# A chunked linear recurrence with both heads of a pair on the partition halves: one state scan, one masked copy, 64x64 matmuls, and two PSUM banks as one buffer

## The chip, the cores and the metric

The kernel runs on one core of one Trainium2 chip. The metric is the device time of the whole launch in microseconds (us), as a median over runs. Engines are named as in the profile: PE is the tensor engine's matmuls, PEld its weight loads, DVE the vector engine, ACT the scalar engine, POOL GpSimd, SP the queue that issues DMAs. L393 is line 393 of the kernel before.

## The reference

A recurrence over 768 time steps (batch 4, 8 heads of 48 columns) feeds a causal attention layer with four experts, of which each token uses two.

```python
for t in range(S):                                   # S = 768, D = 48
    cur = einsum('bhd,bhe->bhde', u[None] * kt, vt)
    y[:, :, t] = einsum('bhd,bhde->bhe', rt, state + cur)
    state = wt[:, :, :, None] * state + einsum('bhd,bhe->bhde', kt, vt)
x = y.transpose(0, 2, 1, 3).reshape(B, S, H * D)     # [4, 768, 384]
logits = x @ w_gate; topk = the two largest; w = softmax over the two
for e in range(4):
    q, k, v = x @ wq[e], x @ wk[e], x @ wv[e]        # 64 columns each
    a = softmax of the causal scores q k' / 8
    out += (gate of e, if chosen) * (a @ v @ wo[e])
```

## The kernel before

**Staging.** A unit is one batch and one half (g = 0 or 1) of its 768 steps: eight units. For each unit `rwkv` computes the recurrence and leaves its output, transposed and split into two parts (`xh`, `xl`); `moe` then does the attention of that half's queries. The recurrence of a unit is meant to run beside the attention of the unit before it. `rwkv` handles the heads in four pairs per unit, so 32 pairs in all, and cuts a half sequence into six chunks of 64 steps.

**Order.** Nothing is issued in program order. Every step is put into a `Plan` with an expected cost per engine, the tiles it reads and writes, and a wanted time (`want`, shifted by a table `OFF`). `Plan.order` then lets each engine take, of the steps whose inputs and buffers are free, the one that is wanted first, and emits the instructions in the order so found. Each engine executes its own list in that fixed order and waits on semaphores. All loads and stores are issued by SP, in order. Buffers are counted in `BUFS`; PSUM has eight banks: `sc` two buffers of two banks (scores), `mo` two of one bank (attention), `rw` two of one bank (recurrence). In the last unit's attention, when no recurrence is left, `mbank` hands out `rw` buffers as well as `mo` buffers, alternately.

**One pair, before** (all in `rwkv`). Head 0 lies on partitions 0 to 47, head 1 on 64 to 111 of a column-per-token layout. `suf` (L345) and `pre` (L349) are scans over the decays on 128 partitions. `kt` (L354) is the decayed keys. `mr` (L358) multiplies the receptances into `pre` twice, each time for 64 partitions: head 0 into the tile `pre`, head 1 into `mB`. `ktp` (L383) transposes the keys on PE and `kts` copies them to SBUF. `aps` (L393, L394) is twelve 64x64 products, two heads by six chunks: head 0's rows go to the lower half of one bank's partitions and head 1's rows to the upper, that is each head crosses to the other half. `am` (L397) copies them with the causal mask, head 0's to the free half of `pre`, head 1's to the free half of `mB`: two DVE instructions of 64 partitions. So `pre` holds, one above the other, what head 0 multiplies with the state and with the values, and `mB` the same for head 1.

`ups` (L409, L410) is what each chunk adds to the state: two blocks (`a` = 0, 1, the partition half of the tokens), each with a bank of its own and six products, and `us` copies each bank to `ust`. `ys` (L417) scans the state over the chunks, one DVE scan per head: into the upper or lower part of `ysA` and `ysB`, whose other part holds the values, laid out to match and loaded from `vY` by two DMAs. `carry` (L421, L424) hands the last state to the other half (g = 0, a DVE copy per head) or clears it (g = 1, a POOL memset per head). `yps` (L433, L434) is the output: twelve products with all 128 (or 112) rows, which read `ysA` and `ysB` with a step of eight floats per column. `addy` (L441) adds it to `xn`. After four pairs, `xp` (L454) transposes `xn` in three steps, each with a bank of `rw`. A product of float32 operands appears in the trace as two weight loads and two matmuls, so twelve products are 24 matmul rows.

Of the kernel before, what the change touches and what calls it, by code (L numbers as in the profile page):

```python
# [20 lines left out]
C = 64  # L21
# [9 lines left out]
# Time of an instruction by its shape, in ns: what the order of the instructions is planned with.  # L31
# [16 lines left out]
class Slot:  # L48
    """A buffer of a tag; which one, the plan says. It is made when the first instruction that needs it is emitted."""
# [11 lines left out]
# Time from the end of an instruction to the start of one on another engine that waits for it.  # L61
# [5 lines left out]
class Plan:  # L67
    """Orders instructions: each engine takes, of those whose inputs and tiles are there, the one that is
    wanted first. The instructions are then emitted by the time at which they started."""
# [5 lines left out]
    def add(self, kind, engs, fn, r=(), w=(), want=None):  # L75
        """engs: {engine: ns}; fn(engine) emits. r, w: what is read and written, Slots or (Slot, part)."""
# [23 lines left out]
    def order(self, free, slack=60.0, width=40):  # L100
# [7 lines left out]
        bufs = {}       # tag -> for each buffer, by when each engine is through with it; None while held  # L108
# [15 lines left out]
        while len(done) < len(ops):  # L124
            best = None
            for e in engines:
                c, t0 = [], 1e30
                for want, n in cand[e][:width]:
                    o = ops[n]
                    t = max(free[e], after(o["ready"], e))  # L130
                    for s in o["slots"]:
# [6 lines left out]
                        elif s.bank:        # two engines don't use a bank at once  # L138
                            t = max(t, after(s.ends, e, e))
# [42 lines left out]
def rwkv_moe(ctx: ExitStack, tc: tile.TileContext, wkr, vY, nat, uN,  # L182
# [12 lines left out]
    def bank(tag, name, dt=F32):  # L195
        w = 2048 // mybir.dt.size(dt) * (2 if tag == "sc" else 1)
        return Slot(ps, [128, w], dt, BANK.get(tag, tag), name, True)
# [26 lines left out]
    act = cst.tile([128, 1], F32, name="act")       # loads the table of the exponential  # L224
# [6 lines left out]
    # the scan over chunks, a row for each column of the state: the state that enters, what the chunks  # L231
    # add, a zero that ends the row; and the decays that follow them
# [25 lines left out]
    sel = cst.tile([NG, 3 * E, HD], BF16, name="sel")   # picks the two experts of a pair out of the gates  # L258
    tri = cst.tile([128, E, E], F32, name="tri")        # [e, e2]: 1 where e2 < e
# [13 lines left out]
    def weights(n, src, cols):  # L273
        """A matrix split exactly into two float32r parts."""
# [12 lines left out]
    def rwkv(b, g, v0, v1):  # L287
# [10 lines left out]
        for p in range(NP):  # L298
# [36 lines left out]
            mB = sb([128, NH, C], F32, "mB", f"mB{n}")  # L335
# [3 lines left out]
            def sfv(suf=suf):  # L339
# [4 lines left out]
            # suffix products inside each chunk, scanned from its end; column 0 of a block: the whole chunk  # L344
# [6 lines left out]
                [(lt, 0), "inv_pre"], [(pre, 0), (pre, 1)])  # L351
# [27 lines left out]
            ktp = bank("rw", f"ktp{n}")  # L379
# [7 lines left out]
            aps = bank("rw", f"aps{n}")  # L387
# [445 lines left out]
```

## Time and profile before

| | before |
|---|---|
| median of 3 runs | 500.53 us (499.93 to 500.97) |
| profiled execution, first to last instruction | 500.3 us |
| PE busy | 450.2 us (90%) |
| DVE busy | 425.7 us (85%) |
| ACT busy | 248.0 us (50%) |
| POOL busy | 170.5 us (34%) |
| mean granted TensorE clock | 0.942 of 2.4 GHz |
| DMA | 46.64 MB, 93 GB/s over the span |

The profiled execution has no time of its own beside its span; the span lies 0.2 us under the median of the timed runs. Busy times count overlapping instructions of one engine once. Matmuls are pipelined: a row's length is its latency, and the distance from one start to the next is what it costs in a stream. The kernel falls into three stretches: a start to about 50 us, a middle in which recurrence and attention run together, and from about 436 us the last unit's attention alone.

### The profile page before, as it was taken

To read this page: it belongs to the slowest core of one execution; us is meant where nothing else is said; L and a number is where in the kernel's file an instruction comes from. 1 tells how busy PE (TensorE), PEld (TensorE's weight loads), DVE (VectorE), ACT (ScalarE), POOL (GpSimd) and SP (SyncE) were. 2 spreads that over 40 slices of the span, in tenths; PEclk is the share of its full clock that TensorE was granted. 3 is DMA by queue.
4 is the path that set the end of the run, shared out by engine and by line. 5 is a ranking of instruction groups with operands and counts; after the bars stand their busy time and mean duration, and the time that the engine had idled before them with its cause. 6 is when DMAs were issued, how large, how long until landed. Compare 5 with 4: busy or idle time off the path is not lost.

```text
span 500.3 us, 10885 instructions
## 1 busy us (share of the span) xinstructions
PE 450.2 (90%) x4191; PEld 332.7 (66%) x4196; DVE 425.7 (85%) x866; ACT 248.0 (50%) x609; POOL 170.5 (34%) x218
## 2 busy tenths in 40 slices
PE   6867797999898998999988988999997989999985
PEld 3545676667766766767766666776766658886654
DVE  7999999969979899989999889989998876766561
ACT  3232545544445644655553734655552734575552
POOL 4555744412454244722234243722233240000000
PEclk9795899959898999999998999999997999999999
DMA  7544534222523323522331233522342110100101
GB/s 243 192 152 137 162 101 137 67 96 67 164 63 103 100 91 92 163 85 69 120 111 64 85 101 99 162 84 70 100 129 64 37 54 17 48 0 1 48 1 47
DMA packets 18564, 46.64 MB, mean 93 GB/s; under 512 B 2512, under 2 KB 9936, under 8 KB 18512
## 3 DMA queue, kind: packets, MB, share of 16 engines
q1 hardware_dynamic: 18512, 45.94, 29.5%
q8 instruction: 33, 0.54, 0.5%
q14 instruction: 19, 0.16, 0.1%
HBM read 41.21 MB, written 4.72 MB: 92 GB/s over the span
## 4 chain that ended last, share of the span: by engine, by line
PE 54%; DVE 34%; issue 5%; DMA 3%; ACT 2%; POOL 1%; SPq 0%; DVEq 0%; ACTq 0%; POOLq 0%
PE sp L589 8%; PE pp L500 7%; PE tp L609 6%; PE sp L588 6%; DVE ysB L417 5%; PE vp L530 4%; DVE pre L349 4%; DVE suf L345 4%; PE yp L632 3%; DVE ysA L417 3%; PE op L696 3%; PE sp L590 3%; PE aps L393 2%; DVE mx L594 2%; PE ups L409 2%
## 5 line engine op out<-in xcount | busy, mean ns | idle before, releaser
L596 ACT ACTIVATE a<-sp,mx 128x512 f32<-128x512 f32 (+5 forms) x96 | 60.8, 634 | 46.8 <-DVE mx L594 40.1
L594 DVE TENSOR_REDUCE mx<-sp 128x1 f32<-128x512 f32 (+5 forms) x96 | 58.8, 619 | 23.4 <-PE sp L590 22.6
L609 PE MATMUL tp<-ident,a 128*128 128x128 f32 x336 | 57.4, 290 | 7.3 <-ACT a L596 4.0
L354 POOL TENSOR_TENSOR kt<-lt,suf 128x384 f32<-128x384 f32 x31 | 33.7, 1087 | 81.8 <-PE aps L394 56.6
L201 ACT COPY ATa<-tp 128x512 f32<-128x512 f32 (+3 forms) x73 | 34.6, 477 | 42.7 <-PE tp L609 42.3
L589 PE MATMUL sp<-KS,QL 64*128 64x384 f32 (+4 forms) x128 | 54.7, 427 | 0.0
L588 PE MATMUL sp<-KS,QD 128*128 128x384 f32 (+4 forms) x128 | 51.4, 402 | 0.8 <-ACT a L596 0.5
L609 PEld LDWEIGHTS tp<-ident,a 128*128 128x128 f32 x336 | 39.2, 146 | 13.7 <-ACT a L596 5.4
L433 PE MATMUL yps<-ysA,pre 128*64 128x48 f32 x384 | 39.6, 276 | 7.9 <-issue 4.6
L500 PE MATMUL pp<-xh,wh_qk 128*128 128x384 f32 x96 | 40.8, 425 | 3.8 <-DVE QL L511 3.8
L374 POOL TENSOR_TENSOR xn<-nat,rk 128x144 f32<-128x144 f32 x42 | 29.9, 720 | 38.8 <-DVE rk L370 38.6
L434 PE MATMUL yps<-ysB,mB 112*64 112x48 f32 x384 | 37.9, 275 | 4.1 <-DVE ysB L417 4.1
L589 PEld LDWEIGHTS sp<-KS,QL 64*128 64x128 f32 x128 | 23.9, 187 | 23.1 <-issue 20.1
L364 POOL TENSOR_TENSOR nat<-nat,u_sb 128x288 f32<-128x288 f32 x30 | 26.6, 886 | 36.5 <-DMA nat<-in_nat_dram 20.7
L433 PEld LDWEIGHTS yps<-ysA,pre 128*64 128x64 f32 x384 | 29.5, 154 | 14.1 <-issue 8.4
L358 POOL TENSOR_TENSOR pre<-lt,pre 64x384 f32<-64x384 f32 x25 | 28.5, 1140 | 26.9 <-DVE pre L349 14.0
L409 PE MATMUL ups<-nat,kts 64*64 64x48 f32 x384 | 33.9, 229 | 2.5 <-DVE mB L397 1.2
L632 PE MATMUL yp<-ATa,v_sb 128*64 128x384 f32 (+2 forms) x224 | 35.9, 449 | 0.1
L345 DVE TENSOR_TENSOR_SCAN suf<-lt,one_suf 128x390 f32<-128x390 f32 x32 | 34.6, 1080 | 1.7 <-DMA lt<-in_wkr_dram 1.3
L509 ACT ACTIVATE QD<-pp 64x384 fp32r<-64x384 f32 x64 | 31.0, 484 | 9.1 <-PE pp L500 7.6
L409 PEld LDWEIGHTS ups<-nat,kts 64*64 64x64 f32 x384 | 26.8, 139 | 13.0 <-issue 6.2
L417 DVE TENSOR_TENSOR_SCAN ysB<-ust,wdec 48x384 f32<-48x384 f32 x32 | 34.6, 1082 | 1.0
(137 smaller groups left out, 1200.0 us busy)
## 6 DMA issues: line engine op xcount, KB each, us to landing
lt<-in_wkr_dram SPq DMA_DIRECT2D x31, 579.5 KB, 3.8
nat<-in_nat_dram SPq DMA_DIRECT2D x32, 432.0 KB, 3.3
out_dram<-ob SPq DMA_DIRECT2D x24, 192.0 KB, 1.9
ysB<-in_vY_dram SPq DMA_DIRECT2D x32, 96.0 KB, 2.5
ysA<-in_vY_dram SPq DMA_DIRECT2D x32, 96.0 KB, 2.6
w_qk<-in_wqk_dram SPq DMA_DIRECT2D x1, 768.0 KB, 4.5
w_vg<-in_wvg_dram SPq DMA_DIRECT2D x1, 390.0 KB, 4.5
lt<-in_wkr_dram SPq DMA_DIRECT2D x1, 384.0 KB, 3.2
```

The lines of the kernel that those rows point to most:

```text
L345: plan.add("suf", {"DVE": t_dve(WB)}, lambda e, suf=suf, w_=w_: nc.vector.tensor_tensor_scan(rev(suf()), rev(w_()), rev(one_suf), 0.0, op0 ...
L409: nc.tensor.matmul(ups()[0:64, o], kts()[q, i, 0:64], vn()[q, i, 0:D], start=True, stop=True)
L417: plan.add("ys", {"DVE": t_dve(D * NX)}, lambda e, rows=rows, ys=ys, us=us, wd=wd: nc.vector.tensor_tensor_scan(flat(ys()[rows]), flat(us[ ...
L433: nc.tensor.matmul(yps()[q, o:o + D], pre()[:, c, 0:C], ysA()[:, :, c], start=True, stop=True)
L434: nc.tensor.matmul(yps()[q, o + D:o + 2 * D], mB()[0:112, c, :], ysB()[0:112, :, c], start=True, stop=True)
L500: nc.tensor.matmul(pp()[:, 0:384], w[:, qk, k, cs], x()[:, k, :], start=(k == j == 0), stop=(k == j == 2))
L588: nc.tensor.matmul(spv()[:, h, :], QD[x]()[:, t], ks[:, o], start=True, stop=False)
L589: nc.tensor.matmul(spv()[:, h, :], QL[x // 2]()[hi, t], ks[hi, o], start=False, stop=h < np_ - 1)
L594: plan.add("max", {"DVE": t_dve(n)}, lambda e: nc.vector.tensor_reduce(mx(), spv(), axis=AX.XY, op=ALU.max, negate=True), [sp], [mx])
L596: plan.add("exp", {"ACT": t_exp(n)}, lambda e: nc.scalar.activation(a()[:, 0:n].rearrange("p (a n) -> p a n", a=np_), spv(), AF.Exp, bias= ...
L609: nc.tensor.transpose(tp()[:, j * 128:(j + 1) * 128], a()[:, (j0 + j) * 128:(j0 + j + 1) * 128], ident)
L632: nc.tensor.matmul(yp()[e * 64:e * 64 + 64, lo:384], v_sb[ep]()[:, j, e * 64:e * 64 + 64], at, start=(j == 0), stop=(j == nj - 1))
```

## The change

Both heads stay on their own partition halves. `mr` becomes one instruction on 128 partitions, in `pre`. `aps` keeps head 0 in the upper and head 1 in the lower half of the partitions; `am` is one instruction of 128 partitions into a tile of its own, `am`. `ups` is one block of twelve products into two banks, its products alternating between the partition halves of the tokens, and `us` one copy of 288 columns instead of two of 144. `ys` is one scan over 112 partitions into one tile, and `carry` one instruction. The values are loaded by one DMA into `vy`, contiguous by chunk. `yps` is 24 products, of 64 (or 48) rows and 64 output rows: for each chunk and head one with the state and one with the values, accumulated in PSUM, head 0 in the first of two banks and head 1 in the second. The recurrence's two one-bank buffers `rw` become one two-bank buffer `rw2`, which `ktp`, `aps`, `ups`, `yps` and `xp` take in turn, and which `mbank` lends out in the last unit. Three planned costs are new constants. `OFF`, `LEAD` and the other tables stay; the planned order follows from the new steps.

```diff
-        w = 2048 // mybir.dt.size(dt) * (2 if tag == "sc" else 1)
+        w = 2048 // mybir.dt.size(dt) * (2 if tag in ("sc", "rw2") else 1)
...
-            ysA = sb([128, D, NX], F32, "ysA", f"ysA{n}")
-            ysB = sb([128, D, NX], F32, "ysB", f"ysB{n}")
-            load("ldv", lambda t=ysB: flat(t()[0:64]), vY[b, g, p, 0:64], -1, [(ysB, "v")])
-            load("ldv", lambda t=ysA: flat(t()[64:128]), vY[b, g, p, 64:128], -1, [(ysA, "v")])
+            ys = sb([128, D, NX], F32, "ys", f"ys{n}")
+            vy = sb([128, NH, D], F32, "vy", f"vy{n}")
+            load("ldv", lambda vy=vy: flat(vy()), vY[b, g, p], NH * D, [vy])
...
-            for rows, m in ((slice(0, 64), pre), (slice(64, 128), mB)):
-                h = rows.start // 64
-                plan.add("mr", prod(384), lambda e, m=m, rows=rows, r_=r_, pre=pre: E_[e].tensor_tensor(
-                    m()[rows, :, 0:C], r_()[rows], pre()[rows, :, 0:C], op=ALU.mult),
-                    [(lt, 1), (pre, h)], [(m, h)])
+            plan.add("mr", prod(384), lambda e, r_=r_, pre=pre: E_[e].tensor_tensor(
+                pre()[:, :, 0:C], r_(), pre()[:, :, 0:C], op=ALU.mult), [(lt, 1), pre], [pre])
...
-                    nc.tensor.matmul(a_[64:128, o], k[0:64, c, :], mA[0:64, c, 0:C], start=True, stop=True)
-                    nc.tensor.matmul(a_[0:64, o], k[64:128, c, :], mB()[64:128, c, :], start=True, stop=True)
-            plan.add("aps", {"PE": 12 * 81}, amat, [kt, (pre, 0), (mB, 1)], [aps])
-            for rows, m, h in ((slice(64, 128), pre, 1), (slice(0, 64), mB, 0)):
-                plan.add("am", {"DVE": t_dve(384)}, lambda e, rows=rows, m=m, aps=aps: nc.vector.tensor_tensor(
-                    m()[rows, :, 0:C], aps()[rows, 0:NH * C].rearrange("p (c j) -> p c j", j=C),
-                    dec_mask[rows, None, :].to_broadcast([64, NH, C]), op=ALU.mult), [aps], [(m, h)])
+                    for h in range(2):
+                        nc.tensor.matmul(a_[half(h), c * C:(c + 1) * C], k[half(h), c, :], m[half(h), c, 0:C],
+                                         start=True, stop=True)
+            plan.add("aps", {"PE": T_APS}, amat, [kt, pre], [aps])
+            plan.add("am", {"DVE": t_dve(384)}, lambda e, am=am, aps=aps: nc.vector.tensor_tensor(
+                am(), aps()[:, 0:NH * C].rearrange("p (c j) -> p c j", j=C),
+                dec_mask[:, None, :].to_broadcast([128, NH, C]), op=ALU.mult), [aps], [am])
...
-            for a in range(2):
-                ups = bank("rw", f"ups{n}{a}")
+            ups = bank("rw2", f"ups{n}")
+            def states(e, ups=ups, kts=kts, vn=vn):
+                for i in range(3):
+                    for a in range(2):
+                        o = slice(a * 512 + i * D, a * 512 + (i + 1) * D)
+                        nc.tensor.matmul(ups()[0:64, o], kts()[half(a), i, 0:64], vn()[half(a), i, 0:D], start=True, stop=True)
+                        nc.tensor.matmul(ups()[64:64 + D, o], kts()[half(a), i, 64:64 + D], vn()[half(a), i, D:2 * D],
+                                         start=True, stop=True)
+            plan.add("us", evac(289), lambda e, ups=ups, us=us: copy(
+                e, us[0:112, :, 1:1 + NH].rearrange("p e (i a) -> p a i e", a=2),
+                ups()[0:112].rearrange("p (a n) -> p a n", a=2)[:, :, 0:3 * D].rearrange("p a (i e) -> p a i e", i=3)),
+                [ups], [ku + ("u",)])
+            plan.add("ys", {"DVE": t_dve(D * NX)}, lambda e, ys=ys, us=us, wd=wd: nc.vector.tensor_tensor_scan(
+                flat(ys()[0:112]), flat(us[0:112]), flat(wd[0:112]), 0.0, op0=ALU.add, op1=ALU.mult),
+                [ku + ("u",), ku + ("in",), kw], [ys])
+            if g == 0:
+                plan.add("carry", {"DVE": 390}, lambda e, ys=ys, us=us: nc.vector.tensor_copy(
+                    us[0:112, :, 0], ys()[0:112, :, NH]), [ys], [ku + ("in",)])
+            else:
+                plan.add("carry", {"POOL": 184}, lambda e, us=us: nc.gpsimd.memset(us[0:112, :, 0:1], 0.0),
+                         [], [ku + ("in",)])
...
+            def outp(e, yps=yps, pre=pre, am=am, ys=ys, vy=vy):
+                for i in range(3):
+                    for part in range(2):
+                        for h in range(2):
+                            o = slice(h * 512 + i * D, h * 512 + (i + 1) * D)
+                            r = slice(0, 64) if h == 0 else slice(64, 64 + D)
+                            for q in range(2):
+                                c = 2 * i + q
+                                if part == 0:
+                                    nc.tensor.matmul(yps()[half(q), o], pre()[r, c, 0:C], ys()[r, :, c],
+                                                     start=i == 0, stop=False)
+                                else:
+                                    nc.tensor.matmul(yps()[half(q), o], am()[half(h), c, :], vy()[half(h), c, :],
+                                                     start=False, stop=i == 2)
...
-        return bank("rw" if spare[0] and spare[1] % 2 else "mo", name, dt)
+        return bank("rw2" if spare[0] and spare[1] % 2 else "mo", name, dt)
...
-BUFS = dict(lt=2, nat=2, ysA=2, ysB=2, suf=2, pre=3, mB=3, kt=2, rk=2, kts=2, xn=2, xh=2, xl=2, lg=2, asum=2, ge=2, m1=2, rank=2, c1=1, c2=1,
+BUFS = dict(lt=2, nat=2, ys=2, vy=2, suf=2, pre=3, am=2, kt=2, rk=2, kts=2, xn=2, xh=2, xl=2, lg=2, asum=2, ge=2, m1=2, rank=2, c1=1, c2=1,
...
-            sc=2, mo=2, rw=2)
+            sc=2, mo=2, rw2=1)
+T_APS, T_UPS, T_YPS = 700, 360, 720
```

Before, the planned costs of `aps`, the two `ups` and `yps` were 972, 2 x 435 and 954 ns.

## Rows read from the trace of the kernel before

**Rows 1.** Busy time by stretch: us, then PE, PEld, DVE, ACT, POOL, clock, DMA.
```profile
0.00:50.00 50.00, 35.56 (x362) 23.06 (x369) 46.20 (x78) 14.35 (x26) 26.84 (x36) 0.80 0.56 181
50.00:425.00 375.00, 346.43 (x3399) 260.21 (x3400) 337.14 (x690) 193.69 (x488) 143.13 (x180) 0.95 0.31 95
...
435.00:475.00 40.00, 39.90 (x239) 28.70 (x237) 24.30 (x64) 23.96 (x61) 0.00 (x0) 1.00 0.06 20
```

**Rows 2.** The chain that ended last: shares by engine, then by line.
```profile
PE 54%; DVE 34%; issue 5%; DMA 3%; ACT 2%; POOL 1%; SPq 0%; DVEq 0%; ACTq 0%; POOLq 0%
PE sp L589 8%; PE pp L500 7%; PE tp L609 6%; PE sp L588 6%; DVE ysB L417 5%; PE vp L530 4%; DVE pre L349 4%; DVE suf L345 4%; PE yp L632 3%; DVE ysA L417 3%; PE op L696 3%; PE sp L590 3%; PE aps L393 2%; DVE mx L594 2%; PE ups L409 2%
```

**Rows 3.** Clock, the view of Rows 1, around its last fall.
```profile
371.56:378.38 6.82, 4.96 (x52) 3.29 (x48) 6.65 (x12) 3.01 (x6) 3.15 (x4) 1.00 0.46 135
378.38:385.20 6.82, 6.11 (x22) 5.50 (x22) 6.09 (x13) 1.90 (x4) 2.20 (x3) 0.50 0.30 106
```

**Rows 4.** State scans (L417), whole span: DVE busy and count, clock, DMA.
```profile
0.00:500.30 500.30, 67.10 (x64) 0.94 0.30 93
```

**Rows 5.** Masked copies (L397), the same view.
```profile
0.00:500.30 500.30, 35.56 (x64) 0.94 0.30 93
```

**Rows 6.** Carries on DVE (L421), the same view.
```profile
0.00:500.30 500.30, 12.34 (x32) 0.94 0.30 93
```

**Rows 7.** Receptance products (L358), the same view: DVE, then POOL.
```profile
0.00:500.30 500.30, 19.91 (x25) 45.39 (x39) 0.94 0.30 93
```

**Rows 8.** Groups by form: busy us, mean ns of one, idle before.
```profile
L345 DVE TENSOR_TENSOR_SCAN suf<-lt,one_suf 128x390 f32<-128x390 f32 x32 | 34.6, 1080 | 1.7 <-DMA lt<-in_wkr_dram 1.3
L458 DVE TENSOR_TENSOR xl<-xp,xh 128x384 fp32r<-128x384 f32 x24 | 12.5, 544 | 1.0 <-ACT xh L456 0.8
L352 ACT COPY wdec<-suf 128x288 f32<-128x288 f32 x32 | 22.5, 704 | 25.6 <-DVE ysB L417 13.7 <-DVE suf L345 11.3
L433 PE MATMUL yps<-ysA,pre 128*64 128x48 f32 x384 | 39.6, 276 | 7.9 <-issue 4.6 <-DVE xn L441 2.6 <-DVE kts L203 0.6
L632 PE MATMUL yp<-ATa,v_sb 128*64 128x128 f32 x32 | 3.1, 273 | 0.0
```

**Rows 9.** Timeline of PE from `aps` into `ups`: start, us, instruction.
```profile
195.93 0.22 PE L394 MATMUL aps<-mB,kt 64*64 64x64 f32 x1
195.93 0.25 PE L409 MATMUL ups<-nat,kts 64*64 64x48 f32 x1
195.98 0.22 PE L393 MATMUL aps<-pre,kt 64*64 64x64 f32 x1
195.99 0.22 PE L394 MATMUL aps<-mB,kt 64*64 64x64 f32 x1
196.02 0.22 PE L409 MATMUL ups<-nat,kts 64*64 64x48 f32 x1
```

**Rows 10.** Timeline around one block of `ups`.
```profile
201.71 0.25 PE L409 MATMUL ups<-nat,kts 64*64 64x48 f32 x1
...
202.19 0.44 PE L500 MATMUL pp<-xh,wh_qk 128*128 128x384 f32 x1
...
202.31 0.47 ACT L201 COPY ust<-ups 112x144 f32<-112x144 f32 x1
```

**Rows 11.** Timeline of PE over one `yps`, after its wait.
```profile
199.25 0.28 PE L434 MATMUL yps<-ysB,mB 112*64 112x48 f32 x1 [0.71 <-DVE ysB L417]
...
200.17 0.36 PE L434 MATMUL yps<-ysB,mB 112*64 112x48 f32 x2
200.45 0.44 PE L696 MATMUL op<-wh_o,yh 128*128 128x384 f32 x1
```

**Rows 12.** Timeline of DVE: the masked copies of the `aps` in Rows 9.
```profile
200.28 0.56 DVE L397 TENSOR_TENSOR pre<-aps,dec_mask 64x384 f32<-64x384 f32 x1
...
201.25 0.54 DVE L397 TENSOR_TENSOR mB<-aps,dec_mask 64x384 f32<-64x384 f32 x1
```

**Rows 13.** Timeline of DVE: the last reads of an `rw` bank by the recurrence.
```profile
435.22 1.02 DVE L458 TENSOR_TENSOR xl<-xp,xh 128x384 fp32r<-128x384 f32 x2 [0.63 <-ACT xh L456]
```

More of the change, by code (lines that the diff above doesn't have):

```diff
@@ L378, in rwkv @@
             kts = sb([128, 3, 128], F32, "kts", f"kts{n}")
-            ktp = bank("rw", f"ktp{n}")
+            ktp = bank("rw2", f"ktp{n}")
             def keysT(e, ktp=ktp, kt=kt):
@@ L402, in rwkv @@
-            for a in range(2):
-                ups = bank("rw", f"ups{n}{a}")
-                def states(e, ups=ups, a=a, kts=kts, vn=vn):
-                    q = slice(a * 64, a * 64 + 64)
-                    for i in range(3):
-                        o = slice(i * D, (i + 1) * D)
-                        nc.tensor.matmul(ups()[0:64, o], kts()[q, i, 0:64], vn()[q, i, 0:D], start=True, stop=True)
-                        nc.tensor.matmul(ups()[64:64 + D, o], kts()[q, i, 64:64 + D], vn()[q, i, D:2 * D],
-                                         start=True, stop=True)
-                plan.add("ups", {"PE": 6 * 72.5}, states, [kts, (na, 0)], [ups])
-                plan.add("us", evac(145), lambda e, ups=ups, a=a, us=us: copy(
-                    e, us[0:112, :, 1 + a:1 + NH:2].rearrange("p e i -> p i e"),
-                    ups()[0:112, 0:3 * D].rearrange("p (i e) -> p i e", e=D)), [ups], [ku + (a,)])
@@ L416, in rwkv @@
-            for rows, ys, h in ((slice(0, 64), ysA, 0), (slice(64, 112), ysB, 1)):
-                plan.add("ys", {"DVE": t_dve(D * NX)}, lambda e, rows=rows, ys=ys, us=us, wd=wd: nc.vector.tensor_tensor_scan(
-                    flat(ys()[rows]), flat(us[rows]), flat(wd[rows]), 0.0, op0=ALU.add, op1=ALU.mult),
-                    [ku + (0,), ku + (1,), ku + ("in", h), kw], [(ys, "s")])
-                if g == 0:
-                    plan.add("carry", {"DVE": 94}, lambda e, rows=rows, ys=ys, us=us: nc.vector.tensor_copy(
-                        us[rows, :, 0], ys()[rows, :, NH]), [(ys, "s")], [ku + ("in", h)])
-                else:
-                    plan.add("carry", {"POOL": 84}, lambda e, rows=rows, us=us: nc.gpsimd.memset(us[rows, :, 0:1], 0.0),
-                             [], [ku + ("in", h)])
@@ L427, in rwkv @@
-            yps = bank("rw", f"yps{n}")
-            def outp(e, yps=yps, pre=pre, mB=mB, ysA=ysA, ysB=ysB):
-                for c in range(NH):
-                    q = slice((c % 2) * 64, (c % 2) * 64 + 64)
-                    o = (c // 2) * 96
-                    nc.tensor.matmul(yps()[q, o:o + D], pre()[:, c, 0:C], ysA()[:, :, c], start=True, stop=True)
-                    nc.tensor.matmul(yps()[q, o + D:o + 2 * D], mB()[0:112, c, :], ysB()[0:112, :, c],
-                                     start=True, stop=True)
@@ L436, in rwkv, with half, amat @@
-            plan.add("yps", {"PE": 12 * 79.5}, outp, [(pre, 0), (pre, 1), (mB, 0), (mB, 1), (ysA, "v"), (ysA, "s"), (ysB, "v"),
-                                             (ysB, "s")], [yps])
+            aps = bank("rw2", f"aps{n}")
+            def half(i):
+                return slice(64 * i, 64 * i + 64)
+            def amat(e, aps=aps, kt=kt, pre=pre):
+                a_, k, m = aps(), kt(), pre()
+                for c in range(NH):
+                    for h in range(2):
+                        nc.tensor.matmul(a_[half(h), c * C:(c + 1) * C], k[half(h), c, :], m[half(h), c, 0:C],
+                                         start=True, stop=True)
@@ new lines, in rwkv @@
+            plan.add("ups", {"PE": T_UPS}, states, [kts, (na, 0)], [ups])
+            plan.add("us", evac(289), lambda e, ups=ups, us=us: copy(
[5 more added lines that the diff above has]
+                [ku + ("u",), ku + ("in",), kw], [ys])
@@ new lines, in rwkv @@
+            if g == 0:
[4 more added lines that the diff above has]
+                         [], [ku + ("in",)])
+            yps = bank("rw2", f"yps{n}")
+            def outp(e, yps=yps, pre=pre, am=am, ys=ys, vy=vy):
[12 more added lines that the diff above has]
+                                                     start=False, stop=i == 2)
@@ L449, in rwkv @@
         for k in range(3):
-            xp = bank("rw", f"xp{b}{g}{k}")
+            xp = bank("rw2", f"xp{b}{g}{k}")
             def xtr(e, xp=xp, k=k):
```

18 lines of the change are left out of this document (7 added, 11 removed).

## The prediction

> **What bounds the kernel now.** Busy time by stretch comes first [rows 1]. In the first 50 us DVE is busy for 46.2 us and PE for 35.6: DVE sets the pace. From 50 to 425 us both are nearly full, PE 346.4 us (92.4%) and DVE 337.1 us (89.9%). From 435 to 475 us, with no recurrence left, PE is busy for 39.90 of 40 us while DVE is at 61%: PE alone is the bound. So PE reaches 99.8% when DVE has room, and loses 7% when DVE has none. The chain that ended last says the same [rows 2]: PE 54%, DVE 34%, and of that the two state scans (L417) are 8%.
>
> The last loss hides in the clock [rows 3]. In the stretch before its last fall PE is busy for 4.96 of 6.82 us and DVE for 6.65 of 6.82; then the granted clock is 0.50 (1.2 GHz in place of 2.4), and PE is busy for 6.11 of 6.82 us with 22 matmuls. A mean of 0.95 over the middle's 375 us [rows 1] is some 37 us at half clock.
>
> **DVE, part by part.** There are 32 pairs.
> - Scans: 64 take 67.1 us, 1.05 us each at 64 or 48 partitions [rows 4]; a scan of 128x390 takes 1.08 [rows 8]. So partitions cost nothing, and 32 scans of 112x384 take 33.6: -33.5 us.
> - Masked copies: 64 take 35.6 us, 0.556 each [rows 5]; a 128x384 instruction that also reads a PSUM tile takes 0.544 [rows 8]. 32 take 17.8: -17.8.
> - Carries: 32 on DVE take 12.3 us [rows 6]; 16 stay: -6.2.
> - Receptance products: 64, of which DVE does 25 in 19.9 us and POOL 39 in 45.4 [rows 7]. Half of each goes: -10.0 on DVE. POOL, at 34%, is no bound.
>
> The sum is 67.5 us, 2.11 per pair. The `addy` keeps its 288 columns, and `us` its total columns, now 288 in one piece: an ACT copy of 288 columns is 0.70 us in the nearest row [rows 8], planned at 0.29, mostly on ACT, which is half idle. One load in place of two shortens SP's list; DMA is at 0.31 in the middle.
>
> **PE, part by part.** The new shapes are not in the trace, so what matters is whether four 64x64 quarters run side by side. Around 195.93 us three do [rows 9]: `aps` runs on in two quarters (L394 starts at 195.93 and 195.99, 0.06 us from matmul to matmul of one quarter) while the first `ups` starts in a third at 195.93 and has its second matmul at 196.02. Nobody slows down. I take four as running freely, 0.06 us per row in each quarter; the other end is two at a time, as within one block today, 0.03 us per row.
> - `aps`: 24 rows in two quarters, as before: 0.
> - `ups`: a block takes from 201.71 to 202.19, 0.48 us with its entry and exit [rows 10], and there are two. Afterwards 24 rows in four quarters, six each: 6 x 0.06 plus 0.12 of entry (0.48 less today's six per quarter) = 0.48: -0.48 per pair; at two at a time 24 x 0.03 + 0.12 = 0.84, -0.12.
> - `yps`: 24 rows take from 199.25 to 200.45, 1.20 us: twelve per column half, the last ending at 200.53, so its start is near 200.26 and the rows of a half are 0.09 apart [rows 11]. A 48-column row lasts 276 ns and a 128-column row of the same array shape 273 [rows 8]. The difference I put down to the operand: `ysA` is read with a step of eight floats. After the change 24 rows still read `ys` so and 24 read `vy` contiguously. Six per quarter at 0.09 and six at 0.06, plus 0.18 of entry and exit: 1.08, -0.12 per pair. If the step costs nothing in quarters, 0.90, -0.30. At two at a time, 24 x 0.045 + 24 x 0.03 + 0.18 = 1.98, +0.78.
>
> On the step the Trainium skill, page "Advanced Engine Details and Errata", section "Memory Cachelines", says that an access pattern that enters a new 16-byte line with each element pays; eight floats are 32 bytes. The trace agrees (0.09 against 0.06 us); by that rule the `yps` stays at 1.08, and without it it would be 0.90, 6 us less in all.
>
> PE: -0.60 us per pair, 19 us in all; the ends are -0.78 (25 us less) and +0.66 (21 us more).
>
> **The new constraint.** `rw` had two buffers, `rw2` is one. A pair uses it for `ktp`, `aps`, `ups`, `yps` and three quarters of an `xp`: 4.75 uses, one after another. A short use is 1.07 us (the `ups` above, 201.71 to the end of its copy at 202.78 [rows 10]). A long one is the `aps` of [rows 9]: its second masked copy ends at 201.79 [rows 12], 5.8 us after its last matmul, because DVE does other work first. The recurrence now reads its last bank at 436 us [rows 13]; in the forecast below that is about 398, 12.4 us per pair, so a use may take 2.6 us. It fits if the masked copies come sooner, which one copy in place of two and a DVE at 75% favour. While a bank is awaited PE has attention work, as long as the unit before has some. I price this at one point of PE's share. What a unit's tail loses is 2 us: the last attention has three free banks in place of four.
>
> **The sum**, from the profiled execution, 500.3 us:
> - Start: four pairs less of 2.11 us are 8.4 us on the bounding engine; some of it is waits for loads: -6.
> - Middle: of 32 pairs in 436 us, 27.5 lie in its 375. PE 346.4 - 27.5 x 0.60 = 330; DVE 337.1 - 27.5 x 2.11 = 279, 74%. Between 92.4% (DVE at 90%) and 99.8% (DVE at 61%), PE's share at 74% is 96% on a line; one point off for the single buffer, 95%. Of the 37 us at half clock a third goes, as DVE leaves fewer gaps; there PE does in 2 us what takes 1: -6. (330 - 6) / 0.95 = 341: -34. At 92.4% and the clock as it is, 357: -18; at 98% with all of the clock back (-19), 317: -58.
> - Tail: +2.
>
> 500.3 - 6 - 34 + 2 = 462 us. Nothing lies around the span (the median of the runs shown is 500.5), so 462 is the forecast; its own range is 440 to 480. The chain gives a check: half of the scans' 8% is 20 us, and as scans are half of what DVE saves (33.5 of 67.5 us), the rest is about 20 more: 40 us, beside the 38 of the sum.
>
> **Rivals.**
> 1. *DVE's time was cover, not bound.* PE's share stays 92.4% and only PE's own 19 us go: 480. For it: PE has 54% of the chain. Against it: the start, and DVE at 97% ahead of the clock's fall. 0.10.
> 2. *Quarters run two at a time.* PE gets 0.66 longer per pair: (346.4 + 18 - 6) / 0.95 = 377, +2; with the start and tail 498. The rows of three quarters speak against it. 0.08. Beside it stands a rule of the Trainium skill, page "TensorEngine Tiling (Array Packing)", section "Performance Considerations": some 60 cycles of overhead per matmul, so that a dimension already small should not be split; by it 24 more rows of `yps` cost 24 x 25 ns = 0.6 us per pair, an estimate from that page, and the time would be near this rival's. The starts of different quarters within 0.01 us [rows 9] do not show such a cost.
> 3. *The single buffer paces the recurrence.* Place: the hand-over of `rw2` from DVE to PE. It decides from 2.87 us per use, 436 / 32 / 4.75, with 64 us of attention behind it. At 2.75 us the time is 32 x 4.75 x 2.75 + 64 + 2 = 484; at 3.0 it is 522, slower. For it: 5.8 us in [rows 12], and planned costs that are short for `us` and `yps`. Against it: short uses of about 1.1 us, and fewer DVE instructions in between. 0.10 for the mild form, 0.10 for the slow one.
>
> **How the numbers follow.** The forecast has 0.62. A change under 0.2% can't be told from none here. Faster: 0.62 + 0.10 + 0.10 of the mild third and half of the second, and a little off for 462's own tail: 0.85. Slower 0.11, same 0.04. The range leaves out the slow form of the third, most of the second and a little below: 438 to 496.
>
> **What would show it.** In the profile afterwards: DVE near 358 us busy with 32 scans of 112x384 near 1.05 us and 32 masked copies near 0.55; `ups` rows in four quarters with 0.06 us from row to row in each, six deep; `yps` blocks near 1.1 us; PE over 94% in the middle; fewer stretches at clock 0.50; the recurrence done by 400 us. The prediction is wrong if a `yps` block takes near 2 us, if POOL, SP or PE wait long for `rw2`'s readers, or if PE's share in the middle stays at 92%.

## The result and the profile after

The changed kernel takes 485.4 us (median of four executions, 481.8 to 490.3) beside 500.2 us for the kernel before on the same chip: a ratio of 0.968, with a 95% interval of 0.962 to 0.974. (Ratios and intervals, here and below, leave out executions that lie over 1.5% above the fastest of the same kernel; medians keep them.) It is faster, by 15 us where 38 were forecast. The profiled execution was the shortest of the four, 481.8 us; its span is 480.1, 1.7 us less, where the forecast took the span for the time.

The first view is the busy time of each engine in three stretches, here cut where the `xp` of the first unit and of the last unit has been read (`xl` at 55 and 413.6 us). Columns as in [rows 1]. The fourth line is the long stretch of half clock at the start.

```profile
0.00:55.00 55.00, 35.92 (x461) 23.47 (x461) 45.98 (x82) 14.02 (x21) 23.64 (x36) 0.72 0.55 184
55.00:414.00 359.00, 335.11 (x4202) 248.10 (x4203) 281.26 (x619) 199.40 (x488) 104.37 (x133) 0.98 0.29 94
414.00:480.10 66.10, 55.25 (x303) 38.23 (x301) 31.14 (x77) 32.27 (x81) 0.00 (x0) 0.96 0.05 19
24.10:51.40 27.30, 16.23 (x284) 13.44 (x285) 21.69 (x37) 6.84 (x11) 12.49 (x13) 0.50 0.45 157
```

The same cut of the kernel before, whose recurrence read these at 52.0 and 436.2 us:

```profile
0.00:52.00 52.00, 37.47 (x387) 24.55 (x392) 48.20 (x81) 15.87 (x28) 28.76 (x37) 0.80 0.55 177
52.00:436.00 384.00, 355.48 (x3483) 267.56 (x3480) 344.01 (x702) 198.84 (x501) 141.75 (x182) 0.95 0.31 94
436.00:500.30 64.30, 57.21 (x330) 40.57 (x326) 33.44 (x85) 33.33 (x80) 0.00 (x0) 1.00 0.06 20
```

The start is 3 us longer (forecast: 6 shorter), the middle 25.7 shorter (forecast 34), the tail 2.4 longer (forecast 2). In the middle DVE has fallen from 90% to 78% of the time, but PE's share has only gone from 92.6% to 93.3%. DVE made room, and PE did not use it.

The chain that ended last, by engine and by line, beside [rows 2]:

```profile
PE 69%; DVE 18%; ACT 4%; DMA 4%; issue 3%; SPq 0%; POOL 0%; DVEq 0%; ACTq 0%
PE sp L597 9%; PE pp L508 9%; PE tp L617 7%; PE yp L640 7%; PE sp L596 6%; PE vp L538 6%; PE op L704 5%; PE aps L395 5%; PE yps L439 4%; PE sp L598 3%; DVE suf L344 3%; DVE pre L348 3%; DMA lt<-in_wkr_dram 2%; PE yps L442 2%; PE ups L409 2%
```

The state scans have left its list of lines. Four lines answer to [rows 4] to [rows 7]; in order they are the state scans (L417), the masked copies (L398), the carries (L421) and the receptance products (L355, DVE then POOL) over the whole span:

```profile
0.00:480.10 480.10, 30.89 (x32) 0.95 0.29 94
...
0.00:480.10 480.10, 17.61 (x32) 0.95 0.29 94
...
0.00:480.10 480.10, 4.44 (x16) 0.95 0.29 94
...
0.00:480.10 480.10, 11.82 (x16) 19.44 (x16) 0.95 0.29 94
```

The timeline of PE over one block of `yps` and one of `ups` (start, us, instruction) answers to [rows 9] to [rows 11]:

```profile
210.10 0.39 PE L439 MATMUL yps<-ys,pre 64*64 64x48 f32 x8
210.29 0.30 PE L442 MATMUL yps<-vy,am 64*64 64x48 f32 x8
210.41 0.36 PE L439 MATMUL yps<-ys,pre 64*64 64x48 f32 x8
210.56 0.31 PE L442 MATMUL yps<-vy,am 64*64 64x48 f32 x8
210.68 0.37 PE L439 MATMUL yps<-ys,pre 64*64 64x48 f32 x8
210.84 0.31 PE L442 MATMUL yps<-vy,am 64*64 64x48 f32 x8
211.09 0.44 PE L617 MATMUL tp<-ident,a 128*128 128x128 f32 x2
...
217.90 0.25 PE L409 MATMUL ups<-nat,kts 64*64 64x48 f32 x1
217.91 0.24 PE L410 MATMUL ups<-nat,kts 64*48 64x48 f32 x1
217.91 0.25 PE L409 MATMUL ups<-nat,kts 64*64 64x48 f32 x1
217.92 0.27 PE L410 MATMUL ups<-nat,kts 64*48 64x48 f32 x2
...
218.18 0.28 PE L409 MATMUL ups<-nat,kts 64*64 64x48 f32 x3
218.39 0.50 PE L596 MATMUL sp<-KS,QD 128*128 128x512 f32 x1
```

Four quarters start within 0.02 us, and 24 rows of `ups` are in and out in 0.49 us (forecast 0.48); 48 rows of `yps` take 0.99 (forecast 1.08). Eight rows that read `ys` with its step of eight floats occupy 0.15 to 0.19 us, eight that read `vy` contiguously 0.12. The mechanism on PE is as forecast.

What isn't, is the hand-over of the one buffer. PE's longest waits by line, the line waited for, the total, the number and the longest:

```profile
PE ups L409 <- DVE am L398: 9.9, 9, 3.1
PE xp L462 <- DVE xl L466: 4.3, 6, 1.4
PE ktp L379 <- ACT ust L201: 3.8, 7, 1.0
PE aps L395 <- DVE xn L448: 3.0, 4, 1.6
```

`ups` reads nothing that `am` writes, `ktp` nothing from `ust`, and `aps` nothing from that `xn`: in each line PE waits for the last reader of `rw2`. The four lines come to 21.0 us, of which some 12 lie before 55 us. The longest wait stands in this start. The timeline of PE there (waits in brackets):

```profile
22.43 0.92 PE L395 MATMUL aps<-pre,kt 64*64 64x64 f32 x24 [1.59 <-DVE xn L448]
23.28 0.60 PE L745 MATMUL warm<-one_suf 128*128 128x512 bf16 x2
26.99 0.34 PE L409 MATMUL ups<-nat,kts 64*64 64x48 f32 x1 [3.11 <-DVE am L398]
```

The second pair's `aps` has to wait 1.59 us until `addy` has read the `yps` before it. It ends at 23.4, DVE masks it at 26.4, and only then may `ups` begin: PE stands still for 3.11 us more. The clock falls to 0.50 at 24.1 us, soon after this second wait begins, and stays there until 51.4. In the stretch just ahead of the fall, which holds the first wait, PE is busy for 1.63 of 3.42 us:

```profile
20.66:24.08 3.42, 1.63 (x27) 0.89 (x26) 3.35 (x8) 0.00 (x0) 1.52 (x3) 1.00 0.81 265
```

With the two banks given out one by one (e1 below), the like stretch of half clock lasts from 28.4 to 45.4 us, 17 us in place of 27.

A count over the timeline gives the price. Between 55 and 414 us the buffer is used 133 times: 28 each of `ktp`, `aps`, `ups` and `yps` and 21 of `xp`. From first matmul to last read it is held for 233.4 us, 1.75 per use; for the other 125.6 us, 0.94 per use, it is empty until the next user's turn in PE's list comes. PE is not idle meanwhile: it stands still for under 5 of these 125.6 us and works for attention in the rest. Together that is 2.70 us per use, where the forecast needed 2.6 and took the shortest use, 1.07, as the sign that there was room. The 2.70 is the middle divided by the uses, since a single buffer is at any time either held or empty; that the buffer costs time has to be shown by other runs.

### The profile page after: what moved, and what is told of

Its sections match the earlier page's. It is cut to its first block, busy times and chain, and to the rows that moved or that the text cites. A ratio compares the mean times of both kernels' runs of the same rounds, so it can differ in the third digit from the quotient of the medians.

```text
span 480.1 us, 12104 instructions
## 1 busy us (share of the span) xinstructions
PE 426.3 (89%) x4964; PEld 309.8 (65%) x4964; DVE 358.4 (75%) x775; ACT 245.7 (51%) x589; POOL 128.0 (27%) x169
## 3 DMA queue, kind: packets, MB, share of 16 engines
q1 hardware_dynamic: 18000, 44.37, 28.4%
## 4 chain that ended last, share of the span: by engine, by line
PE 69%; DVE 18%; ACT 4%; DMA 4%; issue 3%; SPq 0%; POOL 0%; DVEq 0%; ACTq 0%
PE sp L597 9%; PE pp L508 9%; PE tp L617 7%; PE yp L640 7%; PE sp L596 6%; PE vp L538 6%; PE op L704 5%; PE aps L395 5%; PE yps L439 4%; PE sp L598 3%; DVE suf L344 3%; DVE pre L348 3%; DMA lt<-in_wkr_dram 2%; PE yps L442 2%; PE ups L409 2%
## 5 line engine op out<-in xcount | busy, mean ns | idle before, releaser
L602 DVE TENSOR_REDUCE mx<-sp 128x1 f32<-128x128 f32 (+5 forms) x96 | 59.1, 620 | 33.3 <-PE sp L598 32.7
L604 ACT ACTIVATE a<-sp,mx 128x128 f32<-128x128 f32 (+5 forms) x96 | 61.0, 636 | 24.6 <-DVE mx L602 19.8
L353 POOL TENSOR_TENSOR kt<-lt,suf 128x384 f32<-128x384 f32 x29 | 29.1, 1003 | 94.5 <-PE aps L395 78.9
L597 PEld LDWEIGHTS sp<-KS,QL 64*128 64x128 f32 x128 | 23.4, 183 | 22.3 <-issue 19.1
L439 PE MATMUL yps<-ys,pre 64*64 64x48 f32 (+1 forms) x768 | 32.7, 270 | 4.5 <-DVE ys L417 1.7
L201 ACT COPY ust<-ups 112x288 f32<-112x288 f32 x28 | 19.5, 698 | 30.3 <-PE ups L410 30.1
L417 DVE TENSOR_TENSOR_SCAN ys<-ust,wdec 112x384 f32<-112x384 f32 x32 | 30.9, 965 | 5.2 <-ACT ust L201 4.8
L395 PE MATMUL aps<-pre,kt 64*64 64x64 f32 x768 | 30.7, 228 | 3.4 <-DVE xn L448 3.0
L348 DVE TENSOR_TENSOR_SCAN pre<-lt,inv_pre 128x390 f32<-128x390 f32 x32 | 33.2, 1036 | 0.2
L508 PE MATMUL pp<-xh,wl_qk 128*128 128x384 f32 x96 | 33.3, 346 | 0.0
L508 PE MATMUL pp<-xl,wh_qk 128*128 128x384 f32 x96 | 33.2, 346 | 0.0
```

Source lines behind the costliest of these rows:

```text
L201: nc.scalar.copy(o, i)
L348: plan.add("pre", {"DVE": t_dve(WB)}, lambda e, pre=pre, w_=w_: nc.vector.tensor_tensor_scan(flat(pre()), w_()[:, 0:WB - 1], flat(inv_pre) ...
L395: nc.tensor.matmul(a_[half(h), c * C:(c + 1) * C], k[half(h), c, :], m[half(h), c, 0:C], start=True, stop=True)
L439: nc.tensor.matmul(yps()[half(q), o], pre()[r, c, 0:C], ys()[r, :, c], start=i == 0, stop=False)
L508: nc.tensor.matmul(pp()[:, 0:384], w[:, qk, k, cs], x()[:, k, :], start=(k == j == 0), stop=(k == j == 2))
L597: nc.tensor.matmul(spv()[:, h, :], QL[x // 2]()[hi, t], ks[hi, o], start=False, stop=h < np_ - 1)
```

## The experiments

Medians in us; each ratio is to the kernel before, on the same chip (499.6 to 501.8 us). "Merged" is DVE's work as in the change.

| run | DVE's steps | PE's products | buffers of the recurrence | time | ratio, 95% interval |
|---|---|---|---|---|---|
| before | two | as before | two of one bank | 500.2 | 1 |
| after | merged | quarters | one of two banks | 485.4 | 0.968 (0.962 to 0.974) |
| e1 | merged | quarters | the two banks one by one | 466.1 | 0.933 (0.928 to 0.938) |
| e2 | two | quarters | one of two banks | 540.8 | 1.083 (1.077 to 1.089) |
| e3 | merged | as before | two of one bank | 461.8 | 0.925 (0.920 to 0.930) |
| e4 | two | as before | one of one bank | 562.0 | none |
| e5 | merged | quarters | any free one of two banks | 474.3 | 0.947 (0.934 to 0.959) |
| e6 | merged | quarters | two of one bank, and the scores' | 458.5 | 0.919 (0.909 to 0.929) |
| e7 | two | quarters | the two banks one by one | 549.4 | 1.098 (1.087 to 1.109) |
| e8 | merged | two quarters at a time | two of one bank | 500.3 | none |
| e9 | two | quarters | two of one bank, and the scores' | 504.7 | 1.007 (1.003 to 1.011) |
| e10 | merged | quarters, measured costs | one of two banks | 492.6 | 0.980 (0.972 to 0.988) |
| e11 | merged | quarters | one of one bank, and the scores' | 465.9 | 0.935 (0.926 to 0.944) |
| e12 | merged | quarters | as e11, its free bank to attention | 446.7 | 0.893 (0.885 to 0.900) |

For e4 and e8 no ratio was formed: their executions lie far apart (548 to 567 and 488 to 505 us), and in both the shortest stands alone.

### Was it the single buffer?

**e1**, on the kernel after: the two banks are given out one by one. Only `ups` and `yps` take both. Two things change with it. In the last unit both banks are lent out, so that attention has four free banks, as before the change. And `ktp` and `aps` are placed only when the SBUF tile into which they will be copied is free too (also in e5, e7 and e9, not in e6).

```diff
-            ktp = bank("rw2", f"ktp{n}")
+            ktp = half_bank(0)
-            aps = bank("rw2", f"aps{n}")
+            aps = half_bank(1)
-            ups = bank("rw2", f"ups{n}")
+            ups2 = both()
-            yps = bank("rw2", f"yps{n}")
+            yps2 = both()
-            xp = bank("rw2", f"xp{b}{g}{k}")
+            xp = half_bank(k % 2)
```

> The changed kernel with its two PSUM banks given out one by one: the transposed keys take the first, the score products the second, the transposes of the output either, and only the state blocks and the output blocks take both. All engines' work is as in the changed kernel. Theory A, the single two-bank buffer holds PE back: the part of PE's waits in the middle that ends at a reader of that buffer (some 13 of 24 us) and the slow start (3 us longer than before where 6 less was forecast) mostly go: 465 to 474 us. Theory B, DVE's time was cover and PE sets the time: 482 to 488, as the changed kernel.

466.1 us: 19 us come back with the same instructions on PE and DVE. In the profiled spans it is 16.1 us, 3.1 of them in the start, 9.0 in the middle and 4.0 in the tail. Its middle, to the last read of `xp` at 401.6 us:

```profile
52.00:401.60 349.60, 328.29 (x4140) 242.51 (x4140) 285.96 (x630) 194.67 (x479) 102.05 (x128) 0.99 0.31 97
```

The middle is 34.6 us shorter than before, against -34 in the forecast. PE's share is 93.9%, hardly above the 93.3% of the kernel after; most of what the middle gains is busy time of PE (328.3 us in place of 335.1, at a clock of 0.99 in place of 0.98).

**e4**, the other way round, on the kernel before: one buffer in place of two.

```diff
-            sc=2, mo=2, rw=2)
+            sc=2, mo=2, rw=1)
```

> The kernel before with one one-bank recurrence buffer in place of two, nothing else. Theory A: a single buffer costs at least 10 us by itself, 510 to 530 us. Theory B: PE has other work while the buffer is awaited, 500 to 506.

562 us, above both ranges, and 46 more at the least (548.2 against the highest of before beside it, 502.1), with the same instructions. The middle of an execution of 562.4 us:

```profile
64.30:491.50 427.20, 387.73 (x3539) 286.70 (x3539) 339.84 (x699) 206.90 (x519) 123.46 (x168) 0.90 0.27 82
```

PE's share falls to 90.8% of a middle of 427 us, and the clock to 0.90. The kernel before uses the buffer 5.75 times per pair; 28 pairs and 427.2 us make 2.65 us per use; the buffer is held for 301 us, 71% of the middle, beside 65% in the kernel after.

**e5**: any free bank for `ktp`, `aps` and `xp`, where e1 fixes which. The edit is e1's with `half_bank()` for all, and the planner learns to place a step that takes two buffers of one kind.

> As the first experiment, but keys, score products and output transposes take whichever of the two banks is free; state blocks and output blocks still take both. If what is left above 462 us in the first experiment (466) is the fixed choice of a bank, 460 to 463; if it is that two steps still need both banks at once, 464 to 468.

474.3 us, above both ranges: over half of e1's gain. A bank of their own for the keys and for `aps` is the better rule here.

**e6**: `ups` and `yps`, which need two banks, take one of the scores' two two-bank buffers; the rest has two one-bank buffers.

```diff
-            ups = bank("rw2", f"ups{n}")
+            ups = bank("sc2", f"ups{n}")        # likewise yps
-            ktp = bank("rw2", f"ktp{n}")
+            ktp = bank("rw", f"ktp{n}")         # likewise aps, xp
-BANK = {'s1': 'sc'}
+BANK = {'s1': 'sc', 'sc2': 'sc'}
-            sc=2, mo=2, rw2=1)
+            sc=2, mo=2, rw=2)
```

> The changed kernel with state blocks and output blocks in the two two-bank buffers of the scores, and keys, score products and transposes in two one-bank buffers as before. The recurrence's own buffers are then as free as before; the scores have to share. If only the recurrence's buffers matter: 458 to 465 us. If the scores' buffers are as tight: 470 to 485.

458.5 us. Its timeline shows what a second buffer is for; PE's rows of one `aps`, of the two blocks of `ups` and `yps` after it, and of the next `ktp`, and then DVE's masked copy:

```profile
143.16 0.85 PE L395 MATMUL aps<-pre,kt 64*64 64x64 f32 x21
...
145.23 0.25 PE L409 MATMUL ups<-nat,kts 64*64 64x48 f32 x1
...
147.00 0.39 PE L439 MATMUL yps<-ys,pre 64*64 64x48 f32 x8
...
148.70 0.49 PE L379 MATMUL ktp<-ident,kt 128*128 128x128 f32 x3
```

```profile
149.91 0.55 DVE L398 TENSOR_TENSOR am<-aps,dec_mask 128x384 f32<-128x384 f32 x1
```

The `aps` waits 5.8 us for its reader, as long as the one in [rows 12], and PE has meanwhile done four other blocks of the recurrence. Over the middle an `aps` here waits 2.7 us on average from its last matmul to its copy, in the kernel after 0.84 (28 each). So the single buffer did bring the masked copies sooner, as the forecast hoped; it did so because the order had no other choice.

**e10**: on the kernel after, only the planned costs become those that the trace shows.

```diff
-T_APS, T_UPS, T_YPS = 700, 360, 720
+T_APS, T_UPS, T_YPS = 760, 470, 960
-            plan.add("us", evac(289), lambda e, ...
+            plan.add("us", {"ACT": 700, "DVE": 680}, lambda e, ...
```

> The kernel after with its single two-bank buffer, and only the planner's costs changed to what the trace shows: aps 760, ups 470, yps 960 ns of TensorE (700, 360, 720 in the kernel after) and 700 and 680 ns for the copy of the state sums (the same formula as any copy of 289 elements there). If the single buffer itself holds the kernel up, it stays within 478 to 492 us. If what is lost against the forecast is an order planned on costs that are 150 to 240 ns too low, some 15 us come back: 475 us or less.

492.6 us, 0.6 above what was expected if the costs don't matter, and no gain. Planned costs that are too short are not where the time went.

**e11** and **e12**, on e6: one small buffer in place of two, and then the freed bank for attention.

```diff
-            sc=2, mo=2, rw=2)
+            sc=2, mo=2, rw=1)     # e11
+            sc=2, mo=3, rw=1)     # e12
```

> The kernel of the run that takes the scores' two-bank buffers for ups and yps, with one one-bank buffer instead of two for ktp, aps and xp. In the kernel after, the single buffer is used 4.75 times per pair and a use takes 2.70 us of the middle's time (359 us for 133 uses); here it is used 2.75 times per pair. If what counts is the number of uses of the single buffer times about 2.7 us, its uses take 32 x 2.75 x 2.7 = 238 us, far below the middle's 343 us, and the time stays near that of two buffers: 455 to 470 us. If a single buffer costs in itself (its masked copy has to follow at once, whatever the count), most of the 27 us are lost again: 475 to 500 us.

> The same with the bank that this leaves free given to attention (three buffers mo instead of two). If one small buffer costs little, 445 to 462 us, the best version so far; if it costs much, the third attention buffer makes up a part of it only, 465 to 490 us.

465.9 and 446.7 us. One small buffer with 2.75 uses per pair costs 7 us against e6, the one of the kernel after with 4.75 uses costs 27: the price is larger with more uses, and isn't nothing where they lie far below the middle's length. In e11 the buffer is held for 152 us, 43% of the middle, and empty for 2.6 us per use, so a whole turn is 4.6 us there; 2.70 is no constant of a use. The bank that this frees is worth 19 us in attention's hands. e12 beats both kernels, by some 54 and 39 us. Its middle and all of its span:

```profile
45.40:385.10 339.70, 327.47 (x4174) 246.44 (x4175) 290.67 (x624) 193.14 (x481) 112.08 (x144) 0.98 0.32 101
...
PE 413.7 (93%) x4964; PEld 305.6 (68%) x4964; DVE 363.0 (81%) x773; ACT 240.7 (54%) x584; POOL 133.5 (30%) x176
```

### Which half of the change gains?

**e3**, on the kernel before: DVE's steps merged, PE and buffers untouched. The products keep their shapes and number, head 1's reading loaded values where its state would stand, and 48.98 MB are loaded in place of 46.64.

```diff
-            for rows, m in ((slice(0, 64), pre), (slice(64, 128), mB)):
-                plan.add("mr", ... m()[rows, :, 0:C], r_()[rows], pre()[rows, :, 0:C] ...
+            plan.add("mr", ... pre()[:, :, 0:C], r_(), pre()[:, :, 0:C] ...
-            for rows, m, h in ((slice(64, 128), pre, 1), (slice(0, 64), mB, 0)):
+            # am, ys and carry: one instruction of 128 or 112 partitions each
```

> The kernel before with only DVE's steps merged to one instruction per pair; the products on PE, their PSUM banks and two one-bank buffers as before. It leaves out head 1's state (the loaded values stand in its place) and part of the masks, so only its time counts. Theory A: DVE's 67 us less are worth most of the forecast gain without the new buffer: 470 to 482 us. Theory B: 492 to 500, since PE's work is unchanged.

461.8 us, below the range of Theory A: DVE's part alone gives 38 us, more than the whole change.

```profile
44.80:397.30 352.50, 339.11 (x3489) 256.57 (x3490) 289.86 (x635) 196.11 (x496) 108.93 (x138) 1.00 0.35 107
...
PE 427.9 (93%) x4191; PEld 317.5 (69%) x4196; DVE 364.1 (79%) x790; ACT 244.5 (53%) x602; POOL 133.5 (29%) x173
```

The same 4191 matmul rows as before are 427.9 us of PE in place of 450.2, because the clock is 0.983 in place of 0.942 (busy time times clock is 421 and 424); in the middle PE reaches 96.2%.

**e2**, on the kernel after: `mr`, `am`, `ys` and `carry` as two instructions each again, **e7** the same with e1's banks (lent out to attention later in the last unit), **e9** the same with e6's.

```diff
-            plan.add("am", ... am(), aps() ...
+            for h in range(2):          # likewise mr, ys and carry
+                w = slice(64 * h, 64 * h + 64)
+                plan.add("am", ... am()[w], aps()[w] ...
```

> The changed kernel with DVE's steps cut in two again (receptance products, masked copies, state scans, carries: two instructions of 64 or 48 partitions each), PE and PSUM as changed. Theory A: PE's 19 us are gained, the single buffer costs more than that because its readers come later: 500 to 515 us. Theory B: DVE's 67 us are worth little, so 485 to 492.

> Only PE's part of the change: the changed products in 64x64 quarters, but DVE's steps cut in two as before, and the two banks given out one by one as in the first experiment (in the last unit they are lent out later). By the forecast's sum PE's 19 us less are worth 15 to 20 us: 480 to 485. If DVE's time sets the pace while it is at 90%, PE's share is worth little: 495 to 505.

> The kernel after with the masked copy, the scan, the carry and the receptance product each as two instructions again (VectorE about 424 us busy, as before), ups and yps in the scores' two-bank buffers, and two one-bank buffers for ktp, aps and xp. If what made the two kernels with VectorE's old work and the quarters slow (541 and 549 us) was that ups and yps need both banks at once, this one comes out near the kernel before, 488 to 503 us: TensorE's 19 us less are worth 0 to 12 us beside a VectorE with 424 us of work. If the quarters themselves slow VectorE or TensorE when VectorE is loaded, it stays at 530 us or more.

541, 549 and 505 us; the first lies above both of its ranges, the second far above. The middles of the three, in this order:

```profile
57.60:471.50 413.90, 368.18 (x4208) 268.93 (x4209) 341.64 (x689) 205.38 (x503) 122.70 (x166) 0.91 0.26 82
...
60.70:477.20 416.50, 366.63 (x4164) 270.09 (x4164) 339.73 (x690) 201.23 (x494) 123.14 (x161) 0.87 0.26 81
...
49.90:434.80 384.90, 346.34 (x4166) 256.92 (x4165) 342.95 (x684) 202.18 (x500) 134.16 (x175) 0.92 0.29 90
```

e2 is the best sign that the single buffer sets the pace. With DVE's work in two pieces again the buffer is held for 288.0 us of the middle in place of 233.4, 54.6 us more, and the middle is 55 us longer; the time for which the buffer is empty stays the same (125.7 and 125.2 us). Had attention's work on PE set the pace, one would expect a longer hold to come out of the empty time.

e9 says that PE's part is worth nothing while DVE has its old work (504.7, 1.7 us above the range expected; its middle is 384.9 us, as before's 384.2), unless sharing the scores' buffers costs what it saves, which was not tried on the kernel before. e7 fell outside its expectation: the two banks one by one didn't help there. As e9 has the same instructions on both engines, the 45 us between them come from the buffers (and from the lending in the tail: 74.0 us in e7, 66.3 in e9, from the last read of `xp`). That `ups` and `yps` must find both banks empty at once, and a loaded DVE empties them late, fits; it was not tried by itself.

**e8**, on the kernel after: `ups` is split by token half and `yps` by head, each into one bank, so that no block needs two.

```diff
-            yps = bank("rw2", f"yps{n}")
+            for h in range(2):
+                yps = bank("rw", f"yps{n}{h}")   # ups likewise, for a in range(2)
```

> The changed DVE steps with no step that needs two banks: the state blocks as before, one bank for each half of the tokens, and the output as one block per head, each with a bank of its own; two one-bank buffers as before. PE loses 0.4 us per pair on the state blocks and up to 0.9 on the outputs, DVE some 0.15 on the second addition. If free buffers matter most: 458 to 468 us; if PE's time does: 470 to 485.

500.3 us in the median of ten, above both ranges and no gain left; the shortest took 488.4. The busy time of `yps` in the middle shows where PE pays, in the kernel after and then in e8 (an execution of 504.2 us; PE, PEld, DVE, 28 pairs each):

```profile
55.00:414.00 359.00, 30.55 (x1344) 27.09 (x1344) 12.71 (x28) 0.98 0.29 94
```

```profile
49.00:439.70 390.70, 57.29 (x1344) 50.80 (x1344) 16.83 (x56) 0.93 0.28 88
```

All rows of one head lie on one row half of the array, so a block by head keeps two quarters idle: 2.05 us of PE per pair in place of 1.09. With the halves of `ups` (27.39 us in place of 15.96) that is 38 of the 42 us by which PE is busier in e8's middle (377.1 in place of 334.7). It is the second rival's price of 1.98 us for `yps`, made on purpose; that its 498 us are near too says little, as e8's buffers and `ups` are others.

## Why the prediction was wrong

**The bound.** Right. DVE's time was on the path: e3 gives 38 us with PE's instructions untouched, so the first rival (480 us, DVE as cover) falls.

**DVE's sum.** Right: 425.7 less 67.5 is 358, and 358.4 were measured. The scans fell by 36.2 us (forecast 33.5), the masked copies by 18.0 (17.8), the carries by 7.9 (6.2), the receptance products by 8.1 (10.0). These come to 70; the other instructions took some 3 us more.

**PE's blocks.** Right in the mechanism, and a little more than forecast. From its first row to the next instruction a `yps` takes 0.99 us, where the forecast had 1.20 before and 1.08 after; its busy time is 1.09 (30.55 us for 28) where the same count before gives 1.40 (39.28). A pair thus saves 0.2 to 0.3 us here and not 0.12; on `ups` it saves 0.44 (28.19 us to 15.96) where 0.48 was forecast. From the first row of a `yps` to its last start go 0.84 us (median of 32 blocks); with one more step of 0.06 to 0.09 that is the 0.90 of six rows at 0.09 and six at 0.06. It is the entry and exit that were put too long, at 0.18. The trace thus agrees again with the Trainium skill's rule on memory lines ("Advanced Engine Details and Errata", "Memory Cachelines"). With the Trainium skill's rule of some 60 cycles per matmul ("TensorEngine Tiling (Array Packing)", "Performance Considerations") it does not agree where all four quarters have work: 48 rows in 0.84 us are 0.018 us per row, less than the 25 ns that 60 cycles are by the estimate of the forecast, at 2.4 GHz. The second rival needs the order of e8.

**What PE's part is worth.** Smaller than the sum had it. The middle counted 16.5 us less of PE's work at nearly full value, and let a third of the lost clock return. e3 has none of that work saved and still a middle of 352.5 us, 31.7 shorter: PE's share rises to 96.2% and the clock to 1.00. By the forecast's formula DVE's part alone would have been (346.4 - 6) / 0.95 = 358, 17 shorter. e6, with PE's part too, is 3 us faster than e3, and the intervals of the two overlap. The two parts did not add: with DVE loaded PE's part gave nothing (e9), and with DVE relieved a few us. Both of these runs also make the recurrence share the scores' buffers, so what PE's part is worth without that stays open. That e1's middle is 34.6 us shorter, beside the -34 of the forecast, is luck: a right sum of wrong parts.

**The single buffer.** This is the step that failed: "I price this at one point of PE's share." A point is 3.5 us of the middle (324 / 0.95 less 324 / 0.96). Undone alone, the single buffer gives 19 us (e1) or 27 (e6), and set alone into the old kernel it costs 46 at the least and 62 in the median (e4).

In the middle PE's share came to 93.3% where 95% were forecast, with PE's work near the forecast (335 us; 355.5 less 28 x 0.60 and 6 is 333); that is 8 us. The start is 3 us longer where 6 less were forecast, 9 us off: PE waits there for readers of `rw2`, and the clock stays at 0.50 for 27.3 us. Together that is the difference of the profiled spans, 480.1 against 462; the rest up to 485 is the spread of the executions. e1 gives back the 8 us of the middle (9.0), but only 3 of the start's 9: against before the start is 0 in e1, -7 in e3 and -12 in e6, so that part of it stays open. Even in e1 PE's share is 93.9%. By e1 a point of share was thus not far off; what had no price was the start, and the clock, which is 0.72 there and 0.84 in e1's 52 us.

So the mild form of the third rival happened, at the place that it named. Its 484 us stand beside 485, and its 2.75 us per use beside 2.70; that is one agreement and not two, as 2.70 is the middle divided by its uses, and 2.75 was an example that nothing in the forecast led to: so near a figure is luck. What the forecast argued against it was the length of a short use and a freer DVE, both true. But a use is two times: the 1.75 us that the buffer is held, and 0.94 us until the next user comes up in PE's fixed list, behind attention work. The forecast had no term for the second. That these two set the pace of the middle is argued, from e2 above all; that the single buffer costs the time is shown by e1, e4 and e6. The Trainium skill ("Perfetto Trace Analysis", "Matmuls") wants independent groups of matmuls to rotate through different PSUM banks so that the emptying of one overlaps the next; e1 and e4 put 19 and at least 46 us on it.

**The tail.** +2.4 us against +2; with four free banks again (e1) it is 4 us shorter.

## What to carry to other kernels

Before two small buffers become one large one, count its uses and estimate a whole turn for each: the time held, plus the time until the next user's turn in its engine's list. If the sum comes near the length of the stretch, expect the buffer to set the pace, however short a single use is. Afterwards the two times add up to the stretch in any case; look then at how much of it the buffer is held (71% where one buffer cost at least 46 us, 65% where it cost 19 to 27, 43% where it cost 7). And where two engines are both nearly full, time taken off each needn't add: try each half alone, and try a bank that is left over where the other work waits.

## What was unexpected of the hardware

The same 4191 matmul rows cost PE 450.2 us beside a loaded DVE and 427.9 beside a relieved one (clock 0.942 and 0.983): a change that touches nothing on PE took 22 us off its busy time. In the other direction, one buffer less took the same work to 484.7 us (e4, the execution of 562.4 us, clock 0.874). And 24 rows in four quarters (`ups`) go from first to last start in 0.34 us, 0.015 us per row, as the quarters' starts interleave without a visible cost.
